# A feed-forward block with its gradients on one core: w1 in five loads, six banks for the weight gradients, new orders, and a smaller last tile

## The chip, the core and the metric

The kernel runs on one core of a Trainium2 chip. The core has a matrix engine (TensorE, PE in the profile; its weight loads are PEld), a vector engine (VectorE, DVE), a scalar engine (ScalarE, ACT), a general engine (GpSimd, POOL) and SyncE (SP), which here only issues DMAs. The time is the device time of one execution in microseconds. The kernel before took 267.32 us (median of three runs, 267.25 to 269.15).

## The reference

```python
def forward(x, w1, b1, w2, b2):          # x: 1 x 2048 x 448, w1: 448 x 1792, w2: 1792 x 448
    h = gelu(x @ w1 + b1)                # tanh approximation
    return h @ w2 + b2
out, vjp = jax.vjp(forward, x, w1, b1, w2, b2)
return out, *vjp(grad_out)               # gradients of x, w1, b1, w2, b2; all bfloat16
```

Six results: the output, the gradients of x, of w1 and w2, and of the two biases (sums over the 2048 rows). With u = x w1 + b1 and q = grad_out w2^T the hidden gradient is gh = q gelu'(u); then grad x = gh w1^T, grad w1 = x^T gh, grad w2 = h^T grad_out.

## The kernel before, in words

**Shapes.** The 2048 rows are four blocks of 512. The 1792 hidden columns are 14 tiles of 128, taken two at a time: 7 pairs a block, 28 pairs in all, numbered 0 to 27. Inside a block the hidden dimension lies on the partitions, so x and grad_out are loaded transposed (`xT`, `gT`, two buffers each, X0 to X3 and Y0 to Y3 in the lists), and so is w2 (`w2T`, J0 to J3) and w1 (`w1T`, I0 and I1).

**The work of one pair p.** On TensorE: u p.1 and u p.2 (two runs that together make u for 256 hidden columns), q p.1 and q p.2 (the same for q). The 448 rows of the contraction are 3.5 times 128; so the products are made on two halves of 64 rows of the array at once, and a "run" is a row of slots with one product on each half: 3 slots in a run .1, 4 in a run .2. On ACT and DVE: c p A and c p B evict u's two banks with the bias; g is gelu, s the square, t the tanh (ACT); e, r, y, z, m, n are the elementwise steps of gelu' (DVE), and G p multiplies with q out of its banks and writes gh (DVE).

**The output and grad x.** o b.half (and in block 0 the same in small pieces, p p.i) sums h w2 over the 14 hidden tiles for two row tiles, x b.half sums gh w1^T. Each is cut in pieces of hidden tiles, here 0 to 4, 4 to 9 and 9 to 14, and each piece into a run .1 and a run .2, in which the halves of the array change banks; a run .2 may begin only when the run .1 has ended, and a wait through GpSimd sees to that (`run`, L223). v o b.j and v x b.j evict the results to a staging tile, S stores it.

**Banks.** There are eight PSUM banks: 0 to 3 for o and x, 4 and 5 for u (pairs 1 and 2 use banks 0, 1 and 2, 3), 6 and 7 (`qb`) for q.

**Orders.** Nothing is planned at run time: `PE_ORDER`, `ACT_ORDER`, `DVE_ORDER` and `SP_ORDER` (L91 to L131) are lists written out, one for each engine, and each engine works its list from front to back, waiting where an input or a buffer isn't ready. `UB` (L132) names the scratch buffer that holds u of each pair: 0 to 2 are buffers of their own, 3 to 16 parts of `gh_nat` that are not yet in use.

**The start.** W6 is six products on constants. X0 to X3 on PE transpose the first block's rows, b is added later from B; h0.0 and h1.0 make u of pair 0 in two halves of 256 rows. w1 arrives in four column parts (`W1_COLS`, L304, loaded by L0 to L3; `W1_PART` says which part a pair needs) and its last 64 rows in two parts (R0, R1; R2 and R3 load a copy of other rows for the runs .2). K0 to K3 load w2, part by part. DMAs take a small set of semaphores in turn, and SP waits when the one that is due still belongs to a transfer under way.

**The weight gradients.** h is written to DRAM (H, `hT_dram`) and comes back transposed (`HN`, L719); gh is transposed into `gh_nat` (T). Behind the four blocks come 14 tiles of grad w1 (L745 to L763) and 14 of grad w2 (L797 to L816), each of 16 products of 448 columns that sum over all rows, in one bank each; `next_bank` goes round all eight. x in natural layout (Nx) takes w1's place in SBUF when the last u is done, grad_out (Ng) takes `w2T`'s after the last q, each as one DMA. The bias sums (L766 to L793) run on DVE and GpSimd beside it. The very last tile of grad w2 is made, evicted and stored in two halves of 224 columns.

```python
    W1_COLS = ((0, 256), (256, 512), (512, 1024), (1024, 1792))
    ...
    def next_bank():
        nbank[0] += 1
        return (nbank[0] + 3) % 8
    ...
        halves = [(0, D)] if ft < NF - 1 else [(0, D // 2), (D // 2, D)]
```

Of the kernel before, what the change touches and what calls it, by code (L numbers as in the profile page):

```python
# [116 lines left out]
e3 r3 y3 z3 m3 c7B n3 G1 c8B e4 r4 y4 z4 G2 c9B m4 e5 n4 r5 G3 c10B vo0.2 vo0.3 vo0.0 vo0.1 z5 c11B G4 y5 e6 e7 r6 r7  # L117
m5 z6 z7 y6 y7 n5 m6 G5 m7 c13B n6 n7 e8 r8 y8 z8 G6 m8 e9 vo1.0 r9 vo1.1 z9 G7 c14B vo1.2 vo1.3 y9 n8 e10 G8 m9 r10
y10 z10 n9 e11 r11 m10 z11 c16B G9 y11 n10 e12 r12 m11 c17B z12 y12 G10 n11 m12 c18B n12 e13 r13 y13 z13 G11 m13 c19B
n13 e14 r14 y14 z14 G12 e15 r15 m14 z15 y15 n14 G13 m15 e16 n15 r16 y16 z16 G14 m16 e17 n16 r17 y17 z17 c21B m17 G15  # L120
n17 e18 r18 y18 c22B z18 m18 n18 G16 c23B e19 r19 y19 z19 G17 m19 e20 n19 r20 y20 z20 G18 m20 e21 n20 r21 y21 z21 c24B
G19 m21 e22 n21 r22 y22 z22 c25B m22 vo2.0 vo2.1 G20 n22 vo2.2 vo2.3 e23 r23 y23 z23 c26B G21 m23 e24 n23 r24 y24 z24
c27B m24 n24 G22 e25 r25 y25 z25 m25 n25 G23 e26 r26 y26 z26 m26 G24 n26 e27 r27 y27 z27 m27 n27 G25 vo3.0 vo3.1 vo3.2
vo3.3 G26 G27
# [3 lines left out]
So0.1 So0.0 H10 T4 H11 H12 T5 H13 T6 So1.0 T7 So1.1 H14 T8 H15 Y2 T9 H16 X3 H17 T10 H18 T11 Sx0.0 Sx0.1 H19 T12 H20  # L128
T13 T14 T15 H21 Sx1.0 Y3 T16 H22 Sx1.1 H23 T17 T18 T19 H24 So2.0 H25 T20 So2.1 T21 Nx H26 H27 T22 Sx2.0 Sx2.1 T23 T24
# [28 lines left out]
def make_plan(tc, ctx, x, w1, b1, w2, b2, grad_out, out_0, out_1, out_2, out_3, out_4, out_5):  # L158
    nc = tc.nc
    P = 128  # L160
    _, S, D = x.shape
# [55 lines left out]
    pl = Plan()  # L217
# [85 lines left out]
    W1_PART = (0, 1, 2, 2, 3, 3, 3)  # L303
    W1_COLS = ((0, 256), (256, 512), (512, 1024), (1024, 1792))  # L304
# [381 lines left out]
    def after(o, vs):  # L686
        o["after"] = vs
        return o

    for t in SP_ORDER.split():  # L690
        k, a = t[0], t[1:]
        if t[:2] == "xr":
            LXN(int(t[2]), int(t[3]), "SP")
        elif k in "XY":
            b, *hs = num(a)
            LX(*((x2, xT, "xT") if k == "X" else (g2, gT, "gT")), b, hs or [0, 1])
        elif k in "LRKJI":
# [13 lines left out]


    def MM16(bk, fn, rd, v, n):
        pl.op("PE", f"w{v}", fn, rd, [val(v, ("bank", bk))], n)
# [16 lines left out]
    def next_bank():  # L731
        nbank[0] += 1
        return (nbank[0] + 3) % 8
# [63 lines left out]
    for ft in range(NF):  # L797
        halves = [(0, D)] if ft < NF - 1 else [(0, D // 2), (D // 2, D)]
        for (d0, d1) in halves:
# [6 lines left out]
            MM16(bk, mm, ["gn", ("hn", ft)], ("gw2", ft, d0), ("s448" if len(halves) == 1 else "s224", 16))  # L806
# [5 lines left out]
            if ft == NF - 1:  # L812
                dma("SP", f"gw2l{d0}", out4_v[:, ft, d0:d1], dst, [("wo", ft, d0)], [("o4", ft, d0)], 57344)
# [34 lines left out]
```

## Time and profile before

| what | value |
|---|---|
| median of the runs | 267.32 us (267.25, 267.32, 269.15) |
| the profiled execution | 267.19 us, span 265.4 us |
| granted TensorE clock | 0.998 |
| PE busy | 260.3 us (98%) |
| DVE busy | 206.2 us (78%) |
| ACT busy | 124.5 us (47%) |
| DMA | 46.10 MB, mean 174 GB/s |

The profile is of one execution. Its span goes from the first to the last instruction of the core; the execution's own time is 1.8 us longer. A matmul's end is modelled and matmuls overlap, so two rows that start 0.2 us apart may each be 0.38 us long. A row of the timeline or of the chain gives the start and the length in us, the engine, the line, the tile written and the tiles read, and how many instructions were merged; what stands in square brackets is the idle time ahead of it and what ended that. In the views a tile's buffer number is left out (`bank`, `ub`), `w1f` holds w1 and later x, `w2Tf` holds w2 transposed and later grad_out, `HG` holds h and gh, `TR` the scratch of gelu'. L237 is the product inside `run`, so nearly all products of u, q, o and x have this line; L563 are the transposes of the start, L364 the products on constants, L750 and L804 the weight gradients. L408 is an eviction of u on ACT, L410 one on DVE, L506 a plain DMA, L509 and L518 transposing DMAs, L843 the end of the program.

### The profile page before, as it was taken

The numbers are of one execution on the slowest core, as the hardware profiler recorded it, in microseconds if no ns is written. First come the engines' busy times: TensorE is split into PE (matmuls) and PEld (weight loads), VectorE is DVE, ScalarE is ACT, GpSimd is POOL, SyncE is SP. The second block draws the span as 40 slices with busy tenths as digits, with TensorE's granted clock in tenths as the row PEclk, the third lists the DMA queues.
The fourth block names the chain that finished last, engine by engine and source line by source line (L and its number), as shares of the span: only waits on it lengthen the run. The fifth ranks groups of instructions, "written<-read, shape, count | busy, mean of one in ns | idle before, by whom it ended". The sixth has DMA issues, their size and how long they took to land.

```text
span 265.4 us, 5336 instructions
## 1 busy us (share of the span) xinstructions
PE 260.3 (98%) x2169; PEld 163.8 (62%) x2169; DVE 206.2 (78%) x299; ACT 124.5 (47%) x158; POOL 14.1 (5%) x8
## 2 busy tenths in 40 slices
PE   8899999999999999999999999999999999999995
PEld 4465566666666676677777777775555555555554
DVE  6799699999999999989996987389999995101000
ACT  4799776873987985956556411021122021000001
POOL 0000000000000000000000000000000963000000
PEclk9999999999999999999999999999999999999999
DMA  7999969999999992596358933695787997798321
GB/s 199 298 184 217 151 131 207 300 248 282 209 242 180 224 166 43 130 217 86 87 143 235 271 75 81 86 327 117 155 182 187 131 219 158 168 196 209 103 72 35
DMA packets 119787, 46.10 MB, mean 174 GB/s; under 512 B 96735, under 2 KB 119633, under 8 KB 119762
## 3 DMA queue, kind: packets, MB, share of 16 engines
q1 hardware_dynamic: 119188, 45.43, 78.6%
q8 instruction: 17, 0.28, 0.4%
q10 hardware_dynamic: 574, 0.33, 0.4%
q14 instruction: 8, 0.07, 0.1%
HBM read 7.70 MB, written 14.28 MB: 83 GB/s over the span
## 4 chain that ended last, share of the span: by engine, by line
PE 95%; DMA 3%; DVE 1%; SPq 0%; ACT 0%; issue 0%
PE bank L237 47%; PE qb L237 16%; PE bank L804 12%; PE bank L750 11%; PE qb L750 5%; PE qb L804 4%; DMA w1f<-in_w_dram 2%; DMA TR<-in_x_dram 1%; DVE ub L410 1%; SPq L506 0%; ACT w_sb L809 0%
## 5 line engine op out<-in xcount | busy, mean ns | idle before, releaser
L237 PEld LDWEIGHTS <-HG 64*128 64x128 bf16 x896 | 63.4, 94 | 25.6 <-issue 1.1
L237 PE MATMUL qb<-gT,w2Tf 64*128 64x512 bf16 x392 | 53.7, 376 | 0.0
L237 PE MATMUL bank<-xT,w1f 64*128 64x512 bf16 x378 | 51.0, 376 | 0.7 <-DMA w1f<-in_w_dram 0.7
L237 PE MATMUL bank<-w_sb,HG 64*128 64x448 bf16 x448 | 50.0, 349 | 0.3 <-DVE ub L410 0.3
L237 PE MATMUL bank<-w1T_sb,HG 64*128 64x448 bf16 x448 | 48.6, 349 | 0.0
L466 DVE SCALAR_TENSOR_TENSOR HG<-TR,qb 128x1024 bf16<-128x1024 bf16 x28 | 34.1, 1216 | 10.0 <-PE qb L237 9.7
L237 PEld LDWEIGHTS <-w2Tf 64*128 64x128 bf16 x392 | 27.2, 94 | 13.2
L804 PEld LDWEIGHTS <-HG 128*128 128x128 bf16 x240 | 23.4, 98 | 19.2
L750 PEld LDWEIGHTS <-gh_nat 128*128 128x128 bf16 x224 | 21.8, 98 | 20.6 <-issue 0.4
L237 PEld LDWEIGHTS <-w1f 64*128 64x128 bf16 x378 | 24.6, 94 | 15.6 <-DMA w1f<-in_w_dram 1.2
L451 ACT ACTIVATE TR<-TR 128x1024 bf16<-128x1024 bf16 x28 | 29.3, 1050 | 9.7 <-DVE TR L441 9.6
L804 PE MATMUL bank<-w2Tf,HG 128*128 128x448 bf16 (+1 forms) x176 | 32.3, 344 | 0.0
L750 PE MATMUL bank<-w1f,gh_nat 128*128 128x448 bf16 x160 | 30.8, 353 | 0.0
L773 DVE TENSOR_TENSOR w1T_sb<-w1T_sb,gh_nat 128x1792 f32<-128x1792 f32 x14 | 28.4, 2025 | 0.5
L810 DVE CAST w_sb<-bank 128x448 bf16<-128x448 f32 x5 | 3.1, 624 | 24.2 <-PE bank L804 24.2
L456 DVE TENSOR_SCALAR TR<-TR 128x2048 bf16<-128x2048 bf16 x28 | 19.2, 687 | 3.3 <-ACT TR L451 3.1
L779 POOL PARTITION_ALL_REDUCE w1T_sb<-w1T_sb x1 | 10.7, 10656 | 204.6 <-DVE w1T_sb L777 204.6
L426 ACT ACTIVATE TR<-ub 128x1024 bf16<-128x1024 bf16 x13 | 13.7, 1054 | 12.2 <-DVE TR L461 11.9
L461 DVE TENSOR_TENSOR TR<-TR 128x1024 bf16<-128x1024 bf16 x28 | 19.1, 684 | 0.2
L446 DVE TENSOR_TENSOR TR<-TR,HG 128x1024 bf16<-128x1024 bf16 x28 | 19.0, 682 | 0.0
L426 ACT ACTIVATE TR<-gh_nat 128x1024 bf16<-128x1024 bf16 x15 | 15.6, 1047 | 5.1 <-DVE TR L461 5.1
L421 ACT ACTIVATE HG<-gh_nat 128x1024 bf16<-128x1024 bf16 x15 | 15.7, 1054 | 3.1 <-DVE gh_nat L410 2.8
(49 smaller groups left out, 191.0 us busy)
## 6 DMA issues: line engine op xcount, KB each, us to landing
hT_dram<-HG SPq DMA_DIRECT2D x28, 256.0 KB, 3.5
out_dram<-st SPq DMA_DIRECT2D x16, 224.0 KB, 2.3
w1f<-in_x_dram SPq DMA_DIRECT2D x1, 1792.0 KB, 8.8
w2Tf<-in_grad_out_dram SPq DMA_DIRECT2D x1, 1792.0 KB
out_dram<-w_sb SPq DMA_DIRECT2D x2, 448.0 KB, 2.7
out_dram<-xT SPq DMA_DIRECT2D x2, 384.0 KB, 3.0
w_sb<-in_w_dram SPq DMA_DIRECT2D x1, 672.0 KB, 5.8
w1f<-in_w_dram SPq DMA_DIRECT2D x1, 576.0 KB, 7.2
```

The lines of the kernel that those rows point to most:

```text
L237: m = nc.tensor.matmul(bk_(b)[:, 0:n], lhsT=l, rhs=r, start=st, stop=sp, skip_group_check=True)
L421: pl.op("ACT", f"g{p}", lambda: nc.scalar.activation(out=hblk(p), in_=ubuf(p), func=ACT.Gelu_apprx_tanh), [("ub", p)], [v], ("a1024", 1))
L426: pl.op("ACT", f"s{p}", lambda: nc.scalar.activation(out=TR[p % NTR][:, 1], in_=ubuf(p), func=ACT.Square, scale=sc), [("ub", p)], [v], ("a ...
L446: pl.op("DVE", f"R{p}", lambda: nc.vector.tensor_tensor(out=t[:, 1], in0=t[:, 1], in1=hblk(p), op=ALU.mult), [("r", p), ("h", p)], [val((" ...
L451: pl.op("ACT", f"t{p}", lambda: nc.scalar.activation(out=t[:, 0], in_=t[:, 0], func=ACT.Tanh), [("y", p)], [val(("t", p), ("TR0", p % NTR) ...
L456: pl.op("DVE", f"m{p}", lambda: nc.vector.tensor_scalar(out=t[:], in0=t[:], scalar1=1.0, scalar2=None, op0=ALU.subtract), [("t", p), ("r2" ...
L461: pl.op("DVE", f"n{p}", lambda: nc.vector.tensor_tensor(out=t[:, 0], in0=t[:, 0], in1=t[:, 1], op=ALU.mult), [("m0", p), ("m1", p)], [val( ...
L466: pl.op("DVE", f"G{p}", lambda: nc.vector.scalar_tensor_tensor(out=ghblk(p), in0=t[:, 0], scalar=2.0, in1=qb[:, :, :], op0=ALU.subtract, o ...
L750: nc.tensor.matmul(bk_(bk)[:, 0:D], lhsT=gh_nat[:, st // 4, ft, st % 4, :], rhs=x_nat[:, st, :], start=(st == 0), stop=(st == NS - 1))
L773: nc.vector.tensor_tensor(out=hs3, in0=a, in1=gh_nat[:, st // 4, :, st % 4, :], op=ALU.add)
L779: pl.op("POOL", "gb1", lambda: nc.gpsimd.partition_all_reduce(gb1_w, hsum, channels=P, reduce_op=bass_isa.ReduceOp.add), ["hsc"], ["gb1"], ...
L804: nc.tensor.matmul(bk_(bk)[:, 0:d1 - d0], lhsT=h_nat[ft][:, st, :], rhs=g_nat[:, st, d0:d1], start=(st == 0), stop=(st == NS - 1))
```

## The change

Six things change.

1. w1's third part (columns 512 to 1024) becomes two of 256 columns, so there are five parts; the list of SP loads them as L1, L2, L3, L4.
2. `next_bank` goes round six banks, 0 to 5, and leaves `qb` out.
3. x and grad_out in natural layout come in two and three DMAs.
4. The last tile of grad w2 is cut at column 320: 320 and 128 columns.
5. `UB` uses ten scratch buffers in turn instead of fourteen.
6. All four lists are new. W6 becomes W7. o and x are cut at hidden tiles 6 and 10 instead of 4 and 9. Block 2's o comes before block 1's x. u's two evictions are both on ACT from pair 8 on (in part on DVE before), c2A goes from DVE to ACT, and half of x's evictions go from ACT to DVE. On SP, R1 and K0 come right behind w1's new part, X1 comes ahead of J0 and K3, and the first stores of o come earlier.

```diff
-W6 X0 X1 X2 X3 B h0.0 h1.0 u1.1 u2.1 u1.2 u3.1 u2.2 u3.2 p0.0 p0.1 u4.1 p0.2 p0.3 u4.2 p1.0 p1.1 p1.2 p1.3 p2.0 u5.1
-p2.1 p2.2 u5.2 q0.1 p2.3 p3.0 u6.1 q0.2 u6.2 p3.1 p3.2 p3.3 p4.0 u7.1 p4.1 p4.2 u7.2 p4.3 p5.0 q1.1 p5.1 u8.1 q1.2
-u8.2 p5.2 p5.3 q2.1 u9.1 q2.2 u9.2 p6.0 p6.1 q3.1 u10.1 q3.2 u10.2 p6.2 p6.3 q4.1 u11.1 q4.2 u11.2 o1.0.0.4.1
...
+W7 X0 X1 X2 X3 B h0.0 h1.0 u1.1 u2.1 u1.2 u3.1 u2.2 u3.2 p0.0 p0.1 u4.1 p0.2 p0.3 u4.2 p1.0 p1.1 p1.2 u5.1 p1.3 p2.0
+u5.2 p2.1 p2.2 p2.3 u6.1 p3.0 p3.1 u6.2 q0.1 p3.2 p3.3 q0.2 u7.1 p4.0 p4.1 u7.2 q1.1 p4.2 p4.3 q1.2 u8.1 p5.0 p5.1
+u8.2 q2.1 p5.2 p5.3 q2.2 u9.1 p6.0 p6.1 u9.2 q3.1 p6.2 p6.3 q3.2 u10.1 o1.1.0.6.1 u10.2 q4.1 o1.0.0.6.1 u11.1 q4.2
+u11.2 o1.0.0.6.2 q5.1 u12.1 q5.2 u12.2 o1.1.0.6.2 o1.0.6.10.1 u13.1 q6.1 u13.2 q6.2 o1.1.6.10.1 o1.0.6.10.2
...
 ACT_ORDER = """
-xr01 L0 b1 b2 table X1 X3 c0A0 c0A1 s0 g0 c1A t0 s1 c3A s2 g1 g2 s3 c4B t1 g3 t2 c5A s4 g4 s5 c6A g5 g6 t3 c7A g7 s6
...
+xr01 L0 b1 b2 table X1 X3 c0A0 c0A1 s0 g0 c1A s1 c2A c3A s2 g1 g2 c4A g3 g4 t0 c5A t1 g5 s3 s4 c6A t2 g6 c7A s5 g7 t3
+c8A c8B s6 g8 t4 c9A c9B g9 c10A c10B s7 g10 t5 c11A c11B t6 s8 g11 c12A c12B t7 s9 g12 c13A c13B s10 g13 t8 t9 s11
...
 DVE_ORDER = """
-ident X0 X2 Dx0 b1T c0B0 c0B1 b2c e0 r0 y0 c1B z0 c2A c2B c3B m0 e1 n0 r1 y1 z1 c4A e2 r2 y2 z2 m1 Dg0 n1 c5B m2 n2 G0 c6B
...
+ident X0 X2 Dx0 b1T c0B0 c0B1 b2c e0 r0 c1B z0 y0 c2B c3B e1 r1 y1 e2 z1 r2 c4B z2 y2 Dg0 c5B m0 n0 m1 n1 c6B G0 m2 e3 n2
...
 SP_ORDER = """
-xr12 xr24 R0 L1 R2 L2 K0 K2 R3 L3 R1 K1 Y0 J0 K3 X1 J2 J1 I1 E J3 Y1 I0 X2 H0 H1 H2 H3 H4 H5 H6 H7 H8 T0 T1 T2 H9 T3
...
+xr12 xr24 R0 L1 R2 L2 L3 R1 K0 L4 K1 R3 K2 Y0 X1 J0 K3 J1 J2 E J3 I0 I1 Y1 X2 So0.1 H0 H1 H2 H3 H4 H5 H6 H7 H8 T0 T1
...
-UB = (0, 1, 2, 3, 4, 5, 6, 7, 8, 9, 10, 11, 12, 13, 0, 1, 2, 3, 4, 5, 6, 0, 1, 2, 0, 1, 2, 0)
+UB = (0, 1, 2, 3, 4, 5, 6, 7, 8, 9, 0, 1, 2, 3, 4, 5, 6, 7, 8, 9, 0, 1, 2, 0, 1, 2, 0, 1)
...
-    W1_PART = (0, 1, 2, 2, 3, 3, 3)
-    W1_COLS = ((0, 256), (256, 512), (512, 1024), (1024, 1792))
+    W1_PART = (0, 1, 2, 3, 4, 4, 4)
+    W1_COLS = ((0, 256), (256, 512), (512, 768), (768, 1024), (1024, 1792))
...
+    def rows_nat(tag, dst, src, held):
+        for s0, s1 in (((0, 8), (8, 16)) if tag == "xn" else ((0, 6), (6, 11), (11, 16))):
+            o = pl.op("SP", f"{tag}{s0}", lambda s0=s0, s1=s1: nc.sync.dma_start(
+                out=dst[:, s0:s1, :], in_=src[s0 * P:s1 * P, :].rearrange("(s p) d -> p s d", p=P)), [], [tag], ("dma", (s1 - s0) * P * D * 2, "plain"))
+            after(o, held)
...
-        return (nbank[0] + 3) % 8
+        return (nbank[0] + 3) % 6
...
-        halves = [(0, D)] if ft < NF - 1 else [(0, D // 2), (D // 2, D)]
+        halves = [(0, D)] if ft < NF - 1 else [(0, D - P), (D - P, D)]
...
-                dma("SP", f"gw2l{d0}", out4_v[:, ft, d0:d1], dst, [("wo", ft, d0)], [("o4", ft, d0)], 57344)
+                dma("SP", f"gw2l{d0}", out4_v[:, ft, d0:d1], dst, [("wo", ft, d0)], [("o4", ft, d0)], 256 * (d1 - d0))
```

The order in which the program waits for its last stores has no line of its own in the diff.

More of the change, by code (lines that the diff above doesn't have):

```diff
@@ L705, in make_plan @@
         elif t == "Nx":
-            after(pl.op("SP", "xn", lambda: nc.sync.dma_start(out=x_nat, in_=x2.rearrange("(s p) d -> p s d", p=P)), [], ["xn"], ("dma", S * D * 2, "plain")),
-                  [("w1", i) for i in range(4)] + [("w1r", 0), ("w1r", 1), ("w1f", 0), ("w1f", 1)])
+            rows_nat("xn", x_nat, x2, [("w1", i) for i in range(len(W1_COLS))] + [("w1r", 0), ("w1r", 1), ("w1f", 0), ("w1f", 1)])
         elif t == "Ng":
-            after(pl.op("SP", "gn", lambda: nc.sync.dma_start(out=g_nat, in_=g2.rearrange("(s p) d -> p s d", p=P)), [], ["gn"], ("dma", S * D * 2, "plain")),
-                  [("w2T", i) for i in range(4)])
+            rows_nat("gn", g_nat, g2, [("w2T", i) for i in range(4)])
     def MM16(bk, fn, rd, v, n):
@@ L805, in mm @@
                                      start=(st == 0), stop=(st == NS - 1))
-            MM16(bk, mm, ["gn", ("hn", ft)], ("gw2", ft, d0), ("s448" if len(halves) == 1 else "s224", 16))
+            MM16(bk, mm, ["gn", ("hn", ft)], ("gw2", ft, d0), ("s448" if len(halves) == 1 else f"s{d1 - d0}", 16))
             dst, src = gw2_sb[:, ft, d0:d1], bk_(bk)[:, 0:d1 - d0]
```

51 lines of the change are left out of this document (25 added, 26 removed).

## The prediction

> **What bounds the kernel now.** I read the page's first rows, then the chain that ended last, then the busy time by stages.
>
> ```profile
> span 265.4 us, 5336 instructions
> ...
> PE 260.3 (98%) x2169; PEld 163.8 (62%) x2169; DVE 206.2 (78%) x299; ACT 124.5 (47%) x158; POOL 14.1 (5%) x8
> ```
> ```profile
> 4.13 5.08 DMA w1f<-in_w_dram
> ...
> 12.50 1.41 DVE ub L410 x2
> ...
> 13.96 7.34 PE bank L237 x71
> ...
> 169.98 0.86 PE qb L237 x8
> 170.84 6.62 PE bank L237 x70
> ...
> 183.62 6.05 PE qb L750 x32
> ```
> ```profile
> 13.96:177.47 163.51, 163.51 (x1624) 112.94 (x1624) 147.55 (x233) 103.16 (x122) 0.00 (x0) 1.00 0.84 180
> 177.47:262.36 84.89, 84.89 (x464) 45.18 (x464) 48.25 (x36) 12.38 (x25) 13.53 (x2) 1.00 0.71 154
> ```
>
> The first block says that TensorE is busy 98% of the span. The chain (start, length, who) says more: from 13.96 us to the last tile it is TensorE alone. Two pieces before that are not: a DMA of w1 that holds TensorE until 9.26, and two DVE evictions that hold it from 12.50 to 13.96. The third block gives the stages (length, then busy time of PE, PEld, DVE, ACT, POOL; the 1.00 is the granted clock): 163.51 us for u, q, o, x, 84.89 us for the weight gradients, PE busy in all of both.
>
> Is that busy time all work? 8 products of q.2 run two at a time, so 0.86 us is 4 slots, 0.2155 us each; 70 products of 448 columns in 6.62 us are 35 slots of 0.189 us. From p0.0 on there are 448 slots of o and x and 7 for each of 24 u's and 28 q's: 448 x 0.189 + 364 x 0.2155 = 84.7 + 78.4 = 163.1 us of 163.51. So a new order of that stage can win 0.4 us at most; it can lose any amount. What is left to win lies ahead of 13.96 us and behind the last product.
>
> **The change part by part: the start (five parts of w1, new orders).**
>
> ```profile
> 7.71 0.81 PE L237 MATMUL bank<-xT,w1f 64*128 64x512 bf16 x5
> 9.26 0.39 PE L237 MATMUL bank<-xT,w1f 64*128 64x512 bf16 x2 [0.75 <-DMA w1f<-in_w_dram]
> 13.96 0.55 PE L237 MATMUL bank<-w_sb,HG 64*128 64x448 bf16 x4 [0.31 <-DVE ub L410]
> ```
> ```profile
> w1f<-in_w_dram SPq DMA_DIRECT2D x1, 384.0 KB, 5.1
> ```
> ```profile
> 7.98 0.48 DVE L410 TENSOR_SCALAR ub<-bank,b1T 128x256 bf16<-128x256 f32 x1 [0.43 <-PE bank L281]
> ...
> 10.11 0.43 DVE L436 TENSOR_SCALAR TR<-TR 128x1024 bf16<-128x1024 bf16 x1
> 10.45 0.68 DVE L441 TENSOR_TENSOR TR<-TR,ub 128x1024 bf16<-128x1024 bf16 x1
> 11.05 0.75 DVE L410 TENSOR_SCALAR ub<-bank,b1T 128x512 bf16<-128x512 f32 x1
> ...
> 12.49 1.41 DVE L410 TENSOR_SCALAR ub<-bank,b1T 128x512 bf16<-128x512 f32 x2
> ```
> ```profile
> 9.52 1.04 ACT L421 ACTIVATE HG<-ub 128x1024 bf16<-128x1024 bf16 x1
> 10.98 0.69 ACT L408 ACTIVATE ub<-bank,b1T 128x512 bf16<-128x512 f32 x1 [0.42 <-PE bank L237]
> ```
>
> u1.1's last product starts at 8.14 (7.71 + 0.81 less one product of 0.38), so u2.1 could follow at 8.35; it starts at 9.26, when the 384 KB of part 2 have landed (4.13 + 5.1). Afterwards pair 2 needs half of these bytes, and the other half, needed by u3.1 seven slots (1.5 us) later, is part 3. With nothing to wait for, u2.1's next bound is its bank: c0B1 ends at 7.98 + 0.48 = 8.46. With one slow DMA engine the half could still land near 9.2. I take 8.55, near the first end, since half the data is gone.
>
> What is late next? 18 slots of u follow (3.88 us), so TensorE wants p0.0 at 12.43. p0.0 overwrites u2's banks, which c2A and c2B must have emptied. DVE now has c1B, z0, y0, c2B behind r0, which ends at 10.53; following each other with the 0.08 us overlap seen here, c1B ends at 11.2, z0 at 11.9, y0 at 12.5, c2B at 13.15. ACT has c1A, s1, c2A behind g0, which ends at 10.56: c1A to 11.2, s1 (1.05) waits for c1B and ends at 12.35, c2A at 12.95. So p0.0 starts at 13.2 in place of 13.96: DVE, not w1, sets it, and part of the 0.7 us won from the DMA is lost there. Moving c2A to ACT, so that the two evictions no longer follow each other on DVE, matters as much as the DMA. **-0.75 us**; with part 2 no earlier than 9.22 the same sum gives 13.6 (-0.35), with nothing late at all 13.1 (-0.85).
>
> ```profile
> 0.76 2.72 PE L364 MATMUL qb<-const-bfloat16-1.0 128*128 128x512 bf16 x6 [0.76 <-PEq L832]
> ...
> 3.74 1.67 PE L563 MATMUL bank<-st,TR 128*128 128x128 bf16 x16 [0.26 <-DVE st L557]
> ```
>
> The extra wake product (W7) adds at most 2.72 / 6 = 0.45 us behind 3.48, and the transposes wait for DVE until 3.74: 0 to 0.2 us on them. I take 0, since products overlap; and u2.1 waits for w1 whatever they do.
>
> **The loads behind it.** One more w1 load is one more issue on SP ahead of everything else, and X1 is moved ahead of J0 and K3.
>
> ```profile
> 2.25 0.58 SPq L506 DMA_DIRECT2D w1f<-in_w_dram  x1
> ...
> 8.70 5.74 SPq L518 DMA_TRANSPOSE gT<-in_grad_out_dram  x1
> 14.49 1.29 SPq L518 DMA_TRANSPOSE w2Tf<-in_w_dram  x1
> ...
> 21.66 3.97 SPq L518 DMA_TRANSPOSE w2Tf<-in_w_dram  x2
> ```
> ```profile
> DMA to landing us min/median/max: 4.2/4.4/4.5
> ```
>
> The last row is that of J0, J1, J2. The set ahead of J1 stays the same (Y0, X1, J0, K3 in another order), so J1 moves only by the new issue, 0.58 us. J1's own landing no view gives: its issue with J2's takes 21.66 to 25.63, J2's part is 1.30, so J1's ends at 24.3; J0 lands 2.9 us after its issue ends, which puts J1 at 27.2, and 4.4 us from its beginning would be 26.1. Afterwards 26.7 to 27.8. Who waits: q1.1, which comes behind p0.0 at 13.2 + 18 p's of two slots (6.8) + u4 to u7 and q0 (5 x 1.51 = 7.5) = 27.5. So 0 to 0.3 us; I take **+0.1**. X1, J0 and K3 have 0.3 to 4 us to spare by the same sum.
>
> **The long stage.** u's two halves are from pair 8 on both evicted by ACT, and half of x's evictions go from ACT to DVE. By the lists that is 18 casts more and 8 copies fewer on ACT.
>
> ```profile
> L408 ACT ACTIVATE gh_nat<-bank,b1T 128x512 bf16<-128x512 f32 x17 | 11.4, 682 | 4.3 <-PE bank L237 4.2
> ```
> ```profile
> 91.99 1.26 ACT L408 ACTIVATE gh_nat<-bank,b1T 128x512 bf16<-128x512 f32 x2
> ```
>
> ACT gets 18 x 0.68 = 12.2 us on 103.2 of 163.5, 71%, less the 8 copies; DVE gets lighter by about as much. Neither becomes the bound by its sum. Two casts in a row on ACT take 1.26 us (before's c20A, c20B). The tightest place is like u10.2, q4.1, o1.0.0.6.1, u11.1: 3 x 0.2155 + 6 x 0.189 = 1.78 us between u10's end and u11's first write, less 0.16 us for the last product to run out, 0.1 for two signals and 1.26: 0.25 us to spare, if ACT stands waiting. Counted along the lists the other u's and q's have as much or a little less, as they have now. Splitting o and x at 6 and 10 in place of 4 and 9 gives the same slots and as many runs; second halves still follow their first by at least 0.378 us of other work, as p1.2 does now without a wait. Ten scratch buffers in place of fourteen free part of gh_nat earlier. **0**, between -0.4 (above) and what the last rival says.
>
> **The weight gradients.** Six banks in turn: a bank comes back after 6 x 3.03 = 18 us, its eviction takes 0.5 us. The third tile now meets bank 0 (x3's) 6 us after 177.47 and no longer G27's. x_nat in two parts and g_nat in three are three issues of 0.4 us more, and 1792 KB each land as before in
>
> ```profile
> w1f<-in_x_dram SPq DMA_DIRECT2D x1, 1792.0 KB, 8.8
> ```
>
> 8.8 us. x_nat is issued once u27.2 has read w1 and wanted only by the first weight gradient; all of x2's second half, o3 and x3 lie between and cover it. g_nat's issues stand before T27, which waits for G27 anyway. **0**; without the cover it would be 0.4 us per issue.
>
> **The end (320 and 128 columns, order of waits).**
>
> ```profile
> 5.14 0.28 PE L563 MATMUL bank<-st,TR 128*128 128x128 bf16 x2
> ```
> ```profile
> 5.08 0.34 PE L563 MATMUL bank<-st,TR 128*128 128x128 bf16 x3
> ```
> ```profile
> 256.26 4.56 PE qb L804 x32
> 260.83 1.55 PE bank L804 x16
> ```
> ```profile
> L809 ACT CAST w_sb<-bank x6: 345/532/532, 223.0 to 262.4; 128x448 bf16<-128x448 f32 x5, 128x224 bf16<-128x224 f32 x1
> ```
> ```profile
> L843 SPq EVENT_SEMAPHORE  x5: 27/28/28, 264.3 to 264.6; - x5
> ```
>
> A product of 224 columns costs 1.55 / 16 = 0.096 us; with 448 at 0.189 the slope is 0.000415 per column, so 320 cost 0.136 and 128 0.057. That the small one isn't held by its weight load is seen in the transposes: three against two products of 128x128 with weights of their own differ by 0.06 us (the last three, at the full clock). 16 x (0.136 + 0.057 - 2 x 0.096) = 0. The last cast: 0.532 at 448 and 0.345 at 224 give 0.265 at 128, **-0.08**.
>
> ```profile
> hT_dram<-HG SPq DMA_DIRECT2D x28, 256.0 KB, 3.5
> ...
> out_dram<-ub SPq DMA_DIRECT2D x1, 0.9 KB
> ```
>
> After the last store has landed SP goes through five waits about 0.06 us apart before it drains. If the last store's is the last of them, four pass earlier: **-0.25**. Nothing in the diff says so; but by the trace's instructions the DMAs take eight semaphores in turn; the counts of the view of DMA issues, whose first and last rows stand here, add up to 156 = 19 x 8 + 4, and four are added (one of w1, one of x, two of grad_out), so the last one moves from the fourth to the eighth, which is what would do it. Bounds 0 and -0.25.
>
> The Trainium skill, "TensorE: Matmul & The Clock Gate", section "Back-to-back issue gap", speaks against the 128 columns: in a stream of weight load and product it gives about 81 ns each at 128 columns. Estimated by that figure, the last part costs 16 x 0.024 = 0.38 us more and the whole sum below is 0.38 us later; the transposes' 0.06 speaks for the shorter.
>
> **The sum.** -0.75 + 0.1 + 0 + 0 - 0.33 = -1.0 us. The profiled execution took 267.19 us, of which 1.8 lie outside its span; the median is 267.32, 0.13 above. From the median: **266.3 us**.
>
> ```profile
> L804 PEld LDWEIGHTS <-HG 128*128 128x128 bf16 x240 | 23.4, 98 | 19.2
> ```
>
> **Rivals.** (1) The gains come only in part: w1's half is held by a slow engine (-0.35), J1 costs 0.3, the waits at the end keep their places (-0.08): -0.1, 267.2 us. For it: the 5.1 us landing of part 2, long against its bytes; against: the halves land in order. (2) The small products are bound by their weight loads, 98 ns each in the row above: 16 x 0.041 = +0.66, 267.0 us. Against it, the transposes. (The page's rule is of this kind and smaller.) (3) Slower: ACT, taken by both halves of u, answers late. The place is c(p)A in the ACT list behind a 1.05 us activation; a cast that begins more than 0.25 us late holds u(p+1).1 for the rest, up to 0.8 us, and since TensorE has no idle time it is never made up. From 1.0 us in all on, so with two full misses among 20 pairs or four of 0.25, the change is slower; five full ones give +4 - 1 = 270.3, a likelier four halves +1.6 - 1 = 267.9. For it: strict order and a margin of 0.25 us; against: ACT at 71%, and margins of the same size without one wait of PE in the long stage now.
>
> **How the numbers follow.** Forecast (265.7 to 266.9) 0.55; rivals 1 and 2, and mixtures about 267, 0.25; rival 3 0.18, of which a third over 1%; more than forecast 0.02. 1% is 2.7 us, about what a measurement can tell from no change, so nearly all of this is "same": the most that all ends together can win is 0.85 + 0.4 + 0.33 = 1.6 us, 265.7, and a little scatter below that. The range goes from 265.4 to 268.0.
>
> **What would show it.** PE after u1.1: u2.1 at 8.4 to 8.7 and no wait for w1; p0.0 near 13.2 still waiting for DVE. q1.1 waiting for w2Tf by 0.3 us at most. No PE wait for ACT casts between 14 and 177 us; x3 ending near 176.8. The last 16 products 0.057 us apart, and the drain of SP right behind the last landing. The prediction is wrong if TensorE shows waits for L408 in the long stage, or if u2.1 still starts after 9 us.

## The result and the profile after

The changed kernel takes **266.10 us** in the median of 10 runs (265.73 to 266.58), the kernel before, beside it on the same chip, 267.34 in 10 runs (267.12 to 269.15): a ratio of 0.9936 with a 95% interval of 0.9913 to 0.9958. That is -1.24 us, 0.5%: small, but the interval lies below 1. The forecast was 266.3. Its profiled execution has a span of 264.2 us against 265.4.

The page's first rows, then the stages (length, then busy time of PE, PEld, DVE, ACT, POOL):

```profile
span 264.2 us, 5339 instructions
...
PE 260.4 (99%) x2170; PEld 182.7 (69%) x2170; DVE 198.9 (75%) x289; ACT 130.6 (49%) x168; POOL 14.1 (5%) x8
```
```profile
0.00:12.99 12.99, 11.84 (x82) 6.07 (x83) 9.50 (x30) 7.86 (x12) 0.53 (x6) 1.00 0.85 237
12.99:176.64 163.65, 163.65 (x1625) 131.97 (x1625) 136.83 (x223) 110.18 (x133) 0.00 (x0) 1.00 0.83 183
176.64:261.55 84.91, 84.90 (x465) 44.66 (x464) 52.60 (x38) 12.29 (x23) 13.53 (x2) 1.00 0.68 152
261.55:264.20 2.65, 0.00 (x0) 0.00 (x0) 0.00 (x0) 0.27 (x1) 0.00 (x0) 1.00 0.16 43
```

From p0.0 to the last product TensorE is busy without a hole, as before, and the weight gradients take 84.91 us in place of 84.89. So the gain lies at the two ends, as forecast. First the start, as the chain of waits and TensorE's timeline show it:

```profile
0.76 3.14 PE qb L365 x7
3.90 1.53 PE bank L564 x16
...
11.31 1.06 ACT TR L427
12.37 0.58 ACT ub L409
...
12.99 1.05 PE bank L238 x8
```
```profile
3.74 1.70 PE L564 MATMUL bank<-st,TR 128*128 128x128 bf16 x16
...
7.73 4.87 PE L238 MATMUL bank<-xT,w1f 64*128 64x512 bf16 x41
12.99 1.05 PE L238 MATMUL bank<-w_sb,HG 64*128 64x448 bf16 x8 [0.39 <-ACT ub L409]
```

No DMA of w1 stands in the chain any more, and 41 products of u follow each other from 7.73 on. Where before's chain ended in two DVE evictions it now ends in one of ACT (c2A, 12.37 to 12.95), and TensorE works without a hole from 12.99 on (13.96 before), after one wait of 0.39 us instead of one of 0.75 and one of 0.31. The first product of p0.0 is the one that waits for c2A. The second, on the other half of the array, writes u2's other bank and waits for c2B on DVE:

```profile
12.34 0.74 DVE L411 TENSOR_SCALAR ub<-bank,b1T 128x512 bf16<-128x512 f32 x1
```

c2B ends at 13.08, and that product starts at 13.13. The same work done is the fairer measure: u4.1, which follows p0.0 and p0.1 in both kernels, starts at 13.79 in place of 14.61. The end, by the chain, by the groups of the casts, and by SP's waits between 263.0 and 263.6 us:

```profile
254.88 6.67 PE bank L809 x51
261.55 0.02 issue
261.57 0.27 ACT w_sb L814
```
```profile
L814 ACT CAST w_sb<-bank x9: 265/532/532, 222.2 to 261.6; 128x448 bf16<-128x448 f32 x7, 128x320 bf16<-128x320 f32 x1, 128x128 bf16<-128x128 f32 x1
```
```profile
L848 SPq DRAIN  x2: 7/10/13, 263.4 to 263.5; - x2
L848 SPq EVENT_SEMAPHORE  x1: 28/28/28, 263.3 to 263.3; - x1
```

The last cast takes 0.265 us (0.345 before), and where SP went through five waits behind the last landing, one is left: the last store lands at 263.32, and the drain is at 263.40 (264.31 and 264.64 before). From TensorE's end to the span's end there are 2.63 us in place of 3.03 (to 264.18 and 265.41).

One thing has to be known for the rest. The start of h0.0 differs from one profiled execution to the next (5.39 to 6.15 us). x's rows and the 0.9 KB of b2 land at different times, and the full TensorE clock comes at different times. TensorE's transposes in the repeated kernel before (b_again) and in a_w6_8banks, a kernel of the experiments below, wait for no load:

```profile
3.74 1.38 PE L563 MATMUL bank<-st,TR 128*128 128x128 bf16 x16 [0.26 <-DVE st L557]
```
```profile
3.74 1.87 PE L564 MATMUL bank<-st,TR 128*128 128x128 bf16 x16 [0.26 <-DVE st L558]
```

In the second they start 0.107 us apart to the end, in the first the last eight start 0.056 us apart. By the traces' records of the granted clock the full clock begins between 3.42 and 5.80 us, at 5.62 in a_w6_8banks. So I measure from h0.0's first product: to the first weight-gradient product (column "middle"), from there to the last product's start, and from that to the span's end ("end"). By the start times in the traces these are so steady that 0.05 us can be told apart (the middle is 170.91 or 170.92 us in five kernels). There is one profiled execution a row:

| kernel | median us (runs) | ratio to before, 95% | h0.0 at | u2.1 behind it | u4.1 behind it | middle | end |
|---|---|---|---|---|---|---|---|
| before | 267.34 (10) | | 5.64 | 3.63 | 8.98 | 171.76 | 3.31 |
| before again (b_again) | 266.93 (1) | | 5.53 | 2.88 | 8.79 | 171.57 | 3.32 |
| after | 266.10 (10) | 0.9936, 0.9913 to 0.9958 | 5.66 | 2.88 | 8.13 | 170.92 | 2.87 |
| a_w1four | 266.09 (4) | 0.9955, 0.9938 to 0.9972 | 5.66 | 2.97 | 8.13 | 170.92 | 2.92 |
| a_c2dve | 266.68 (10) | 0.996, 0.9928 to 0.9993 | 6.15 | 2.88 | 8.79 | 171.57 | 2.86 |
| a_w1four_c2dve | 267.01 (10) | 0.997, 0.994 to 0.9999 | 5.94 | 2.88 | 8.79 | 171.57 | 2.92 |
| a_actextra | 266.65 (10) | 0.997, 0.9955 to 0.9985 | 5.74 | 2.88 | 8.17 | 171.42 | 2.87 |
| a_tail224 | 266.61 (7) | 0.9945, 0.9914 to 0.9977 | 6.13 | 2.88 | 8.13 | 170.91 | 3.07 |
| a_onenat | 266.41 (4) | 0.9957, 0.994 to 0.9974 | 5.88 | 2.88 | 8.13 | 170.91 | 3.04 |
| a_w6_8banks | 266.83 (10) | 0.998, 0.9942 to 1.0018 | 5.85 | 2.88 | 8.13 | 170.92 | 3.23 |
| v_start | 266.01 (4) | 0.9947, 0.9929 to 0.9965 | 5.76 | 2.88 | 7.80 | 170.90 | 2.86 |
| v_k3 | 265.84 (8) | 0.992, 0.989 to 0.995 | 6.00 | 2.88 | 7.80 | 170.50 | 2.86 |
| a_b2late | 265.96 (9) | 0.9932, 0.9906 to 0.9958 | 5.39 | 3.10 | 8.57 | 171.78 | 2.87 |
| v_k3_b2late | 265.80 (7) | 0.9923, 0.9893 to 0.9954 | 5.57 | 3.10 | 8.39 | 171.09 | 2.86 |

The weight gradients, the third part, are 84.70 to 84.74 us in all of them. The medians were taken at four times, at which before had 267.34 to 267.62, and differences between them of 0.1 to 0.3 us are within what they scatter; the columns of the traces decide.

### The profile page after: what moved, and what is told of

It reads as the page before. It is cut to its first block, busy times and chain, and to the rows that moved or that the text cites. A ratio compares the mean times of both kernels' runs of the same rounds, so it can differ in the third digit from the quotient of the medians.

```text
span 264.2 us, 5339 instructions
## 1 busy us (share of the span) xinstructions
PE 260.4 (99%) x2170; PEld 182.7 (69%) x2170; DVE 198.9 (75%) x289; ACT 130.6 (49%) x168; POOL 14.1 (5%) x8
## 4 chain that ended last, share of the span: by engine, by line
PE 97%; ACT 1%; DVE 1%; issue 0%; ACTq 0%; DVEq 0%
PE bank L238 46%; PE bank L755 16%; PE bank L809 16%; PE qb L238 16%; PE qb L365 1%; ACT TR L427 1%; PE bank L282 1%; PE bank L564 1%; DVE ub L411 0%; ACT ub L409 0%; DVE TR L432 0%; DVE TR L437 0%; PE qb L630 0%; ACT w_sb L814 0%; ACTq L427 0%
## 5 line engine op out<-in xcount | busy, mean ns | idle before, releaser
L238 PEld LDWEIGHTS <-HG 64*128 64x128 bf16 x896 | 70.9, 94 | 17.8 <-issue 0.7
L238 PE MATMUL qb<-gT,w2Tf 64*128 64x512 bf16 x392 | 55.9, 376 | 0.0
L238 PE MATMUL bank<-xT,w1f 64*128 64x512 bf16 x378 | 53.4, 376 | 0.0
L809 PE MATMUL bank<-w2Tf,HG 128*128 128x448 bf16 (+2 forms) x240 | 42.6, 340 | 0.0
L755 PE MATMUL bank<-w1f,gh_nat 128*128 128x448 bf16 x224 | 42.5, 352 | 0.0
L238 PEld LDWEIGHTS <-w2Tf 64*128 64x128 bf16 x392 | 32.6, 94 | 8.2 <-issue 0.2
L238 PEld LDWEIGHTS <-w1f 64*128 64x128 bf16 x378 | 31.4, 94 | 8.3 <-issue 0.3
L760 ACT ACTIVATE TR<-bank 128x448 bf16<-128x448 f32 x14 | 7.6, 543 | 34.9 <-PE bank L755 34.9
L815 DVE CAST w_sb<-bank 128x448 bf16<-128x448 f32 x6 | 3.7, 624 | 25.9 <-PE bank L809 25.9
L814 ACT CAST w_sb<-bank 128x448 bf16<-128x448 f32 (+2 forms) x9 | 4.4, 490 | 37.7 <-PE bank L809 37.7
L409 ACT ACTIVATE ub<-bank,b1T 128x512 bf16<-128x512 f32 (+1 forms) x26 | 16.2, 666 | 10.9 <-DVE TR L442 6.0
```

Of the source, the lines that this page charges most:

```text
L238: m = nc.tensor.matmul(bk_(b)[:, 0:n], lhsT=l, rhs=r, start=st, stop=sp, skip_group_check=True)
L409: fn = lambda: nc.scalar.activation(out=out, in_=src, func=ACT.Identity, bias=bias)
L755: nc.tensor.matmul(bk_(bk)[:, 0:D], lhsT=gh_nat[:, st // 4, ft, st % 4, :], rhs=x_nat[:, st, :], start=(st == 0), stop=(st == NS - 1))
L760: fn = (lambda dst=dst, src=src: nc.scalar.mul(out=dst, in_=src, mul=-0.5)) if eng == "ACT" else \
L809: nc.tensor.matmul(bk_(bk)[:, 0:d1 - d0], lhsT=h_nat[ft][:, st, :], rhs=g_nat[:, st, d0:d1], start=(st == 0), stop=(st == NS - 1))
```

## The experiments

All are edits of the kernel after, if nothing else is said, and compute the same outputs.

**Start: w1's parts or the evictions?** My theory was that both carry the 0.75 us, the split about half of it. The rival: one alone. Three kernels undo the one, the other, and both.

a_w1four:
```diff
-    W1_PART = (0, 1, 2, 3, 4, 4, 4)
-    W1_COLS = ((0, 256), (256, 512), (512, 768), (768, 1024), (1024, 1792))
+    W1_PART = (0, 1, 2, 2, 3, 3, 3)
+    W1_COLS = ((0, 256), (256, 512), (512, 1024), (1024, 1792))
 SP: ...
-R2 L2 L3 R1 K0 L4 K1
+R2 L2 R1 K0 L3 K1
```

> The changed kernel with w1 in four parts again (its third part has 512 columns; one DMA fewer), all else kept. Theory (w1's wait and the evictions of u2 each hold p0.0, the later one decides): u2.1 waits for the 384 KB and starts near 9.1 in place of 8.54; u2's banks are free near 13.5 in place of 13.08; u4.1 starts near 14.2 in place of 13.79, the end of x3 is 0.4 us later, and one wait more stands behind the last store (0.06): +0.45 us, some 266.55 us. Rival 'the five parts carry the start alone': all of the 0.83 us comes back. Rival 'the new lists carry it alone': at most 0.1 us comes back.

a_c2dve (a_w1four_c2dve has both edits):
```diff
 ACT: ...
-g0 c1A s1 c2A c3A s2
+g0 c1A s1 c3A s2
 DVE: ...
-c1B z0 y0 c2B c3B
+c1B z0 y0 c2A c2B c3B
```

> The changed kernel with c2A back on DVE, behind y0 and ahead of c2B; w1 in five parts. Theory: u2.1 still at 8.54, but c2A runs 12.34 to 13.08 and c2B to 13.75 on DVE, so the second product of p0.0 starts at 13.8 in place of 13.13: +0.65 us, the time near 266.75, although w1 comes as early as before the edit. Rival 'the five parts carry the start': 0 to +0.1 us.

> Both of these undone at once. Theory (the later of the two holds p0.0): p0.0's second product near 13.95 as in the kernel before, u4.1 near 14.6: +0.83 us and 0.06 for the waits at the end, 267.0 us; less than the sum of the two single edits (0.45 + 0.65). If the two were independent, the sum, +1.1 us, 267.2.

TensorE's timeline behind u1.1, of a_w1four and of a_w1four_c2dve:

```profile
7.73 4.96 PE L238 MATMUL bank<-xT,w1f 64*128 64x512 bf16 x41
13.00 1.05 PE L238 MATMUL bank<-w_sb,HG 64*128 64x448 bf16 x8 [0.30 <-ACT ub L409]
```
```profile
8.01 4.87 PE L238 MATMUL bank<-xT,w1f 64*128 64x512 bf16 x41
13.41 0.35 PE L238 MATMUL bank<-w_sb,HG 64*128 64x448 bf16 x1 [0.53 <-DVE ub L411]
14.07 0.91 PE L238 MATMUL bank<-w_sb,HG 64*128 64x448 bf16 x7 [0.31 <-DVE ub L411]
```

With four parts u2.1 comes 0.09 us later, and p0.0 doesn't notice: its wait is 0.30 in place of 0.39, and the middle has the same 170.92 us. The wait of 0.4 us that I expected did not come, since the 384 KB landed at 8.59 us here. With c2A back on DVE (a_c2dve has the same two waits as the second fence), p0 waits twice, 0.53 and 0.31, and the middle is **0.65 us** longer. The two edits together are not longer than c2A alone, where I had expected 0.83. So the place of c2A gives 0.65 us, and the split gives 0 in executions in which w1 lands as it did here.

**Was w1 late in the kernel before?** Its profiled execution said so. The same kernel, profiled again:

> The kernel before once more, for its start alone. If the landing of w1's 384 KB at 9.22 us belongs to that list of loads, u2.1 starts again 3.6 us behind h0.0, with a wait of 0.7; if it was one slow DMA engine of one execution, u2.1 comes 2.9 us behind h0.0 with a wait of 0.1 at most. p0.0 waits for DVE in both.

Its DMA issues and its TensorE timeline:

```profile
w1f<-in_w_dram SPq DMA_DIRECT2D x1, 384.0 KB, 4.1
```
```profile
7.61 4.87 PE L237 MATMUL bank<-xT,w1f 64*128 64x512 bf16 x41
13.01 0.35 PE L237 MATMUL bank<-w_sb,HG 64*128 64x448 bf16 x1 [0.53 <-DVE ub L410]
13.66 0.56 PE L237 MATMUL bank<-w_sb,HG 64*128 64x448 bf16 x4 [0.31 <-DVE ub L410]
```

The 384 KB took 4.1 us in place of 5.1, and TensorE didn't wait for them. What stays are the two waits for DVE, 0.53 and 0.31, the same as in a_w1four_c2dve, and the middle is 171.57, the same again. So the wait of 0.75 us for w1 in the first profile belonged to that one execution. In the four profiled executions that load 384 KB they landed at 9.22, 8.17, 8.59 and 8.32 us (before, b_again, a_w1four, a_w1four_c2dve); how often they are as late as 9.22 four executions can't say, and what the split is worth then no run shows. In the first profile, in the DMA's records, 14 of its 16 engines were done by 8.11 us, one at 8.71 and one at 9.22. Even then it cost 0.19 us of the middle (171.76), because DVE was next. This closes the account of the middle: 0.65 for c2A and 0.19 for the late w1 make the 0.84 us between the two profiled executions, and nothing is left for the new orders of the long stage as a whole.

**Can a late ACT eviction be made up?** The rival that ended on the slower side rested on this. a_actextra makes the square of pair 8 twice on ACT (the second over the first), and so makes c12A and c12B late:

```diff
-    lambda: nc.scalar.activation(out=TR[p % NTR][:, 1], in_=ubuf(p), func=ACT.Square, scale=sc),
+    lambda: [nc.scalar.activation(out=TR[p % NTR][:, 1], in_=ubuf(p), func=ACT.Square, scale=sc)
+             for _ in range(2 if p == 8 else 1)],
```

> The changed kernel with the square of pair 8 (1.05 us on ACT, about 48 us into the span) made twice into the same place, so that the evictions of u12 come 0.95 us later. Theory (the long stage has no spare time, a late eviction beyond its margin is never made up): u13.1 waits by 0.95 less a margin of 0.25 to 0.4, x3 ends 0.55 to 0.7 us later and so does the program: 266.7 us. Rival 'ACT at 71% has time to spare and the loss is made up': 0.

```profile
52.26 0.82 PE L238 MATMUL bank<-xT,w1f 64*128 64x512 bf16 x6 [0.33 <-ACT ub L409]
```

u13.1 waits for ACT, in this row 0.33 us, and the middle is 0.50 us longer: one activation of about 1 us too many costs half of itself, and 120 us of full TensorE behind it give nothing back. Measured from h0.0, c12A starts 0.99 us later than in after. So the mechanism of that rival is real, and the margin at this place is some 0.5 us (0.99 - 0.50), more than the 0.25 that I had. Without the extra work TensorE is never idle in the 163.65 us.

**The end: the parts of the last tile, the waits, the banks.** Three kernels, one for each:

a_tail224:
```diff
-        halves = [(0, D)] if ft < NF - 1 else [(0, D - P), (D - P, D)]
+        halves = [(0, D)] if ft < NF - 1 else [(0, D // 2), (D // 2, D)]
```

> The changed kernel with the last tile in halves of 224 columns. Theory: the products take the same 3.07 us together; the last cast 0.345 in place of 0.265, the last store's landing up to 0.08 us longer: +0.08 to +0.16 us. Rival 'products of 128 columns are held by their weight loads': TensorE ends 0.4 us or more earlier than in the changed kernel, and the time gets shorter.

a_onenat (x and grad_out in natural order by one DMA each, so three DMAs fewer in all):
```diff
-        for s0, s1 in (((0, 8), (8, 16)) if tag == "xn" else ((0, 6), (6, 11), (11, 16))):
+        for s0, s1 in ((0, 16),):
```

> The changed kernel with x and grad_out in natural layout as one DMA each (three DMAs fewer). Theory: the split itself is worth nothing, but the last store now carries the fifth of the eight semaphores in place of the eighth, so three waits more stand between its landing and the drain, 0.06 us each: +0.19 us, all of it behind the last store's landing; x3 and the weight gradients end as they do now. Rival 'the order of the waits has nothing to do with the number of DMAs': 0. Rival 'the split hides part of the loads': the first tile of a weight gradient begins later.

a_w6_8banks:
```diff
-W7 X0
+W6 X0
 ...
-        return (nbank[0] + 3) % 6
+        return (nbank[0] + 3) % 8
```

> The changed kernel with six products on constants at the start and eight banks for the weight gradients, as before the change. Theory: both are worth nothing, the span within 0.1 us of the changed kernel's 264.2. Rival: the seventh product brings the full clock earlier, so the transposes and u2.1 come 0.1 to 0.2 us later here; or qb's banks wait for G27 and the third tile of grad w1 begins later.

The end of a_tail224 is 0.20 us longer; 0.04 of it is the last product itself, since I measure from its start, 0.08 the last cast, shown by the chain, and 0.09 the store, which by the DMA's records takes 1.55 us from issue to landing against 1.46 for 128 columns:

```profile
257.99 4.03 PE bank L809 x37
262.01 0.02 issue
262.04 0.34 ACT w_sb L814
```

In a_onenat the last store has another semaphore, and SP's waits between 263 and 264 us are four behind the landing at 263.53, where after has one; the end is 0.17 us longer, as expected of three more:

```profile
L848 SPq EVENT_SEMAPHORE  x4: 28/28/28, 263.5 to 263.7; - x4
L848 SPq DRAIN  x2: 7/10/13, 263.8 to 263.9; - x2
```

For a_w6_8banks I expected nothing, and the end is **0.36 us** longer. ACT's timeline of the last microseconds, of this kernel and then of after, and this kernel's chain:

```profile
260.87 0.86 ACT L814 CAST w_sb<-qb 128x448 bf16<-128x448 f32 x2 [7.70 <-PE qb L809]
261.76 0.27 ACT L814 CAST w_sb<-bank 128x128 bf16<-128x128 f32 x1
```
```profile
258.51 0.53 ACT L814 CAST w_sb<-bank 128x448 bf16<-128x448 f32 x1 [5.52 <-PE bank L809]
260.68 0.42 ACT L814 CAST w_sb<-bank 128x320 bf16<-128x320 f32 x1 [1.64 <-PE bank L809]
261.57 0.27 ACT L814 CAST w_sb<-bank 128x128 bf16<-128x128 f32 x1 [0.47 <-PE bank L809]
```
```profile
254.88 0.76 PE bank L809 x4
255.63 5.20 PE qb L809 x32
260.83 0.91 PE bank L809 x16
```

In the rotation of eight the last full tile and the 320 columns fall into the two banks of `qb`, which the program holds as one tile. The cast of the last full tile doesn't start when its own 16 products are done (3.0 us into the 5.20) but at the end of all 32, at 260.87, where after starts it at 258.51. Three casts and three store issues are then due within a microsecond: the last store is issued 0.29 us later after TensorE's end than in after, and takes 0.08 us more to land. The kernel before has the same late cast behind its `qb` run of 4.56 us,

```profile
260.86 0.78 ACT L809 CAST w_sb<-qb 128x448 bf16<-128x448 f32 x2 [7.05 <-PE qb L804]
```

and loses nothing by it, because its last half, 1.55 us of products, gives ACT and SP the time. So six single banks are what makes a short last part possible. The weight gradients and the end together are 88.01 us before, or 87.76 without the 0.25 us of waits at its end; 87.78 with the six banks alone (a_tail224), 87.97 with the short last part alone (a_w6_8banks) and 87.61 with both (after). The banks are worth nothing alone and 0.36 us together with the short part, and the short part without them loses 0.2 us. That W6 has no part in the 0.36 is read from the middle and the start, which are as in after.

**Is there more at the start?** v_start puts the evictions c1, c2 and c3 ahead of the elementwise steps of the first pairs on ACT and DVE (up to pair 10 some later entries move by a few places with them):

```diff
 ACT: ...
-g0 c1A s1 c2A c3A s2 g1 g2 c4A g3
+g0 c1A c2A c3A g1 s1 c4A g2 g3 s2
 DVE: ...
-e0 r0 c1B z0 y0 c2B c3B e1 r1 y1 e2 z1 r2 c4B z2 y2 Dg0 c5B
+c1B c2B c3B e0 y0 r0 c4B e1 r1 z0 y1 z1 c5B Dg0 e2 y2
```

> The changed kernel with the ACT and DVE lists of the first pairs reordered: c1, c2 and c3 stand ahead of the elementwise steps of pair 0 and of the squares on both engines (ACT: g0 c1A c2A c3A g1 s1 c4A; DVE: c1B c2B c3B e0 y0 r0 c4B). Theory: after the change p0.0 still waits 0.39 us of PE for u2's evictions, which stand behind s1 and y0 and not behind u2 itself; freed of these they run 11.8 to 12.5, p0.0 starts at 12.6, u4.1 at 13.4: -0.45 us, 265.65 us. Rival: the steps put back come too late for G0, u5.1 or q1.1 and a wait there takes it back: 0 or later than the changed kernel.

u4.1 comes 0.33 us earlier, but the middle is 170.90: the gain is lost at p4.0, which now waits for w2's part 3 (K3), an ordinary load that stands behind the transposing ones of Y0, X1 and J0 on SP's queue and lands at 25.9 us:

```profile
25.95 0.93 PE L238 MATMUL bank<-w_sb,HG 64*128 64x448 bf16 x8 [0.22 <-DMA w_sb<-in_w_dram]
```

So v_k3 is v_start with K3 issued earlier. v_k3_b2late has both of these, and it and a_b2late, which is after with nothing else changed, also move the product of b2 (B), which in several executions waited for its 0.9 KB and held h0.0, behind u1.1:

```diff
 SP (v_k3, v_k3_b2late): ...
-K2 Y0 X1 J0 K3 J1
+K2 Y0 K3 J0 X1 J1
 PE (v_k3_b2late, a_b2late): ...
-X3 B h0.0 h1.0 u1.1 u2.1
+X3 h0.0 h1.0 u1.1 B u2.1
```

> v_start with K3 ahead of J0 and X1 alone. If K3 alone held p4.0, u4.1 stays 0.33 us earlier from h0.0 on and the first gw1 product too: 170.6 us behind h0.0's start in place of 170.9, 265.7 us in all. If the next wait takes it back, 170.8 to 170.9 and 266.0.

> The kernel after with B alone moved behind u1.1. Theory: in the profiled executions so far h0.0 began between 5.64 and 6.15 us, and where it was late, B waited for b2's load; without B ahead of it h0.0 starts at 5.4 to 5.65 us, bound by the copies of x, every time, and u2.1 about 2.9 us later; -0.1 to -0.3 us. Rival: x's own rows are as late as b2, and h0.0 still starts between 5.65 and 6.1 us: 0.

> The kernel after with three things more: c1, c2 and c3 ahead of the elementwise steps on ACT and DVE (as in v_start), w2's part 3 (K3) issued ahead of J0 and X1, and the small product of b2 (B) behind u1.1 instead of ahead of h0.0. If the gain that v_start lost came back only because K3 landed at 25.9 us, K3 now lands before 23 us, p4.0 doesn't wait, and the 0.33 us stay; h0.0, no longer behind b2's load, starts at 5.4 to 5.65 us, 0 to 0.25 earlier. Sum -0.35 to -0.55 against after: 265.6 to 265.75 us. Rival: something else is late next (X1 for u7.1 near 24.6 us, J1 for q1.1 near 27 us, or an eviction), shown by a wait of TensorE behind 13 us; then 265.9 to 266.1.

v_k3's TensorE is not idle ahead of p0.0, u4.1 or p4.0; the last row is DVE's, c3B:

```profile
12.83 1.01 PE L238 MATMUL bank<-w_sb,HG 64*128 64x448 bf16 x8
13.80 0.82 PE L238 MATMUL bank<-xT,w1f 64*128 64x512 bf16 x6
...
25.78 0.94 PE L238 MATMUL bank<-w_sb,HG 64*128 64x448 bf16 x8
```
```profile
12.99 0.75 DVE L411 TENSOR_SCALAR gh_nat<-bank,b1T 128x512 bf16<-128x512 f32 x1
```

Its middle is 170.50, 0.41 us below after's. The column of u4.1 shows 0.33 of it because it takes u4.1's first product, on one half of the array. The other half's first product starts 0.095 us behind that in after and 0.005 in v_k3, so it comes 0.42 us earlier, and this is kept to the end. Evictions still set the start here: u4.1 begins when c3B has ended (13.74), 0.30 us behind the start of the last product of p0. With 265.84 us (265.65 to 266.12) v_k3 is the best kernel together with v_k3_b2late, 0.1% below after; the intervals overlap. With B moved h0.0 starts at 5.39 and 5.57, which is as early as expected, and waits for w1's first part; b_again has 5.53 with B in its place, so that the move brought this is not shown. In the two profiled executions nothing of it is left later on; a_b2late's is the slowest of its nine (266.55 us). TensorE's timeline in a_b2late, then in v_k3_b2late with the row of its DMA issues for w1's last part:

```profile
5.39 2.12 PE L282 MATMUL bank<-xT,w1f 128*128 128x256 bf16 x15 [0.22 <-DMA w1f<-in_w_dram]
...
26.45 0.74 PE L238 MATMUL bank<-w_sb,HG 64*128 64x448 bf16 x6 [0.32 <-DMA w_sb<-in_w_dram]
```
```profile
13.96 0.82 PE L238 MATMUL bank<-xT,w1f 64*128 64x512 bf16 x6 [0.31 <-DMA w1f<-in_w_dram]
```
```profile
w1f<-in_w_dram SPq DMA_DIRECT2D x1, 576.0 KB, 6.8
```

In both u4.1 waits for the last 576 KB of w1, which landed at 13.9 us (12.97 in after, 13.3 in v_k3), and p4.0 of a_b2late for K3. In the medians a_b2late is 0.14 us below after, less than what the runs scatter. Close behind the evictions the next bound of the start are the loads, which came 0.2 to 0.3 us too late for their use in one execution or another.

## Why the prediction was right, step by step

The sum, -1.0, came out at -1.24, and the two profiled executions give the same: -0.84 in the middle and -0.40 at the end. That the medians agree with this so well is in part luck, since 0.19 of the 0.84 is the late w1 of one execution; the rest is 1.05. Inside the start two shares were wrong and nearly cancel, the J1 term was wrong, and the store at the end was not in the sum.

- **The start, -0.75: measured -0.84 (middle), but not by the parts that I named.** u2.1 at 8.54 (I had 8.55, bounded by c0B1), c2A's end at 12.95 (12.95) and c2B's at 13.08 (13.15) came out nearly as worked out; the later of them is DVE's, as I had it, and p0.0's second product starts behind it at 13.13 (13.2). The step that failed is the "0.7 us won from the DMA": I took one execution's wait for a cost of the list of loads, and gave the split 0.4 of the 0.75 us (-0.35 without it). a_w1four shows 0.00 in the middle, and the repeated kernel before shows that the landing at 9.22 was one execution's. The sentence that the place of c2A "matters as much as the DMA" said too little: it carries 0.65, all of it but for that one late landing.
- **W7, 0: right by the columns.** The wake products now run until 3.90 us by the chain without a hole, the transposes start at 3.74 in before, after and a_w6_8banks, and from h0.0 on the last two are alike. What it may do to the scatter stands below.
- **J1, +0.1: 0.** This step rested on a misread list: in the kernel before J2 stands ahead of J1, and the 2.6 us of issue that I gave to J1 were J2's. The change moves J1 ahead of it. SP's timeline, the view of w2Tf from 20 to 21 us, and TensorE's q1.1:

```profile
20.19 4.86 SPq L519 DMA_TRANSPOSE w2Tf<-in_w_dram  x2
```
```profile
DMA to landing us min/median/max: 5.2/5.2/5.2
```
```profile
27.40 0.91 PE L238 MATMUL qb<-gT,w2Tf 64*128 64x512 bf16 x6
```

  In the kernel before J1 was issued at 24.33 and landed at 28.86. Here J1 is issued at 20.19 and lands at 25.34, not 26.7 to 27.8; q1.1 starts at 27.40 (27.5 expected) and doesn't wait.
- **The long stage, 0: right.** From u4.1 to the first weight-gradient product both kernels take 162.8 us (171.76 - 8.98 and 170.92 - 8.13), so the changes of the lists, of scratch buffers and of the split of o and x are together worth nothing to 0.01 us. The margin of ACT was about 0.5, not 0.25 us.
- **Weight gradients, 0: right** (84.70 and 84.74). **Six banks, 0: wrong in combination.** I looked at how late a bank comes back and not at which tile shares `qb`: with the 128 columns the eight banks cost 0.36 us. The sum didn't notice, as the change has both.
- **The end, -0.33: -0.40** (the column's 0.44 less 0.04 of the last product). The cast gave 0.08 and the waits 0.25, as worked out from the count of DMAs. The products of 128 columns cost 0.91 / 16 = 0.057 us each (the chain of a_w6_8banks), as forecast, and start 0.056 us apart in after too, so rival 2 fell; the Trainium skill's 81 ns ("TensorE: Matmul & The Clock Gate", "Back-to-back issue gap") doesn't hold for these 16. Not in the sum: the store of 128 columns lands in 1.46 us, that of 224 in 1.54, another -0.08.
- **The rivals.** Partial gains (267.2) did not occur, and the slow DMA engine that spoke for it turned out to be a matter of the execution. The slower rival's mechanism was shown by a_actextra at 0.50 us for one miss; the lists of the change keep clear of it.

## What to carry to other kernels

A wait that one profiled execution shows for a DMA may belong to that execution: before crediting its removal, look at what is next behind it, and profile the same kernel twice. When TensorE is busy to the end, price an edit by the last wait ahead of the full stretch (here the order of two evictions on two engines, 0.65 us) and by what lies behind the last product; between them there was 0.4 us to win at most, and one late eviction (0.50 us) was not won back. An edit that is worth nothing alone can be what another one needs: the order of banks decides how late the last tiles come to their cast, and the count of DMAs decides which wait is the last.

## What the runs showed that was not expected

**The scatter.** Of 70 executions of the kernel before, over the whole study, 21 took 268.9 to 270.5 us and the others 266.9 to 268.2, with a mean of 268.0 against a median of 267.5. Of 83 executions of after and of the ten kernels made from it that keep seven wake products, none took over 267.4. Of the 10 of a_w6_8banks, 4 took 268.3 to 270.2. So besides 1.2 us in the median the change takes away a jump of 1.5 to 3 us in three of ten executions, worth 0.5 us more in the mean, and undoing the seventh wake product and the rotation of banks brings it back. The two were undone together, and no profiled execution was one of the long ones, so which of them it is, and how, stays open. The granted clock of the views can't tell: it reads 1.00 in the first 13 us of after as well, where a wake product of 512 columns takes 3.14 / 7 = 0.45 us and a later slot of 512 columns 0.2155. The traces' records of the clock say more: the full clock begins at 5.10 us in after, and between 3.42 and 5.80 us in the twelve profiled executions that have such a record, although the first wake product starts at 0.76 in all. I take the wake product for the likelier cause, since without it TensorE stands still for 0.26 us before the first transposes; this is not shown. The Trainium skill ("TensorE: Matmul & The Clock Gate", "Part 1: The HAM clock gate") says that the clock opens only behind a busy window of about 3.4 us and that the windows run free of the kernel's start; estimated from that page, one window more at half the clock would cost 1.7 us. The traces agree with a window of this length: the records of the full clock last 259.41 or 262.83 us, 3.41 apart, and begin at different times. That a long execution misses a window no trace here shows.

**Landing within one DMA.** The same 384 KB took 4.1 us in one execution and 5.1 in another, where two of the 16 engines came late, and the last 576 KB of w1 landed between 12.2 and 13.9 us over the runs. Here a margin under half a microsecond against a load at the start did not hold in every execution.

**The program's last waits** are served one after the other, about 0.06 us each, in the order of the eight semaphores that the DMAs take in turn: 0.33 us with the last store on the fourth, 0.08 on the eighth, 0.27 with three DMAs fewer.
